# The attention output's transposition: TensorE and a copy, or a transposing DMA

## The chip, the cores and the metric

The kernel runs on one core of a Trainium2 chip. The metric is the device time of one execution, in microseconds, and smaller is better. The time before is 302.44 us, the median of three runs (302.19 to 304.47).

## The reference

Inputs are `q`, `k`, `v` of shape 4 x 8 x 768 x 64 (batch, head, position, channel), a small `sort_net` of 4 x 8 x 8 x 8, and the weights of a feed-forward layer. The 768 positions of a head are 8 blocks of 96. Attention runs inside a block; keys and values are first mixed across blocks by a matrix `P`.

```python
P = sort_net
for _ in range(5):
    P = exp(P - max(P, -1)); P = P / sum(P, -1); P = P / sum(P, -2)
k_sorted = einsum('bhij,bhjcd->bhicd', P, k_blocks)
v_sorted = einsum('bhij,bhjcd->bhicd', P, v_blocks)
scores = q_block @ k_sorted_block.T / sqrt(64)
attn   = softmax(scores)
x      = (attn @ v_sorted_block)          # rearranged to 3072 tokens x 512
h      = x @ w_in                         # 512 -> 2048
g      = max(h, 0) + alpha * min(h, 0)
out    = g @ w_out                        # 2048 -> 512, float32
```

## The kernel before

There are 32 attention steps `g`, one for each batch and block, and each step treats 96 tokens for all 8 heads. Batch `b` owns steps 8b to 8b+7. Before a batch can start, its queries, keys and values are loaded by GpSimd's queue (`load_q`, `load_k`, `load_v`), transposed or mixed on TensorE (`prep_q`, `prep_k`, `prep_v`) and copied out of PSUM; values also pass a rearranging copy (`conv_v`). The feed-forward weights come over the same GpSimd queue at the start, between batch 0's and batch 1's data.

One attention step (the function `attention`) is a chain. `s1` (L522) makes the scores, VectorE takes their negated row maximum `nm` (L527), `s2` (L535 and L540) makes the scores again with the maximum subtracted, ScalarE takes the exponential `Esb` (L546), and `o` (L554) multiplies by the values, with a column of ones that gives the row sums. VectorE takes the reciprocals `rec` (L559) and writes the normalised result `xq` (L562): 96 tokens on partitions, 512 channels in bf16 beside one another, 1,024 bytes in a row. There are two buffers of `xq`, used in turn.

The feed-forward layer wants channels on partitions. So four TensorE transposes (L571), one for each group of 128 channels, write into the free half of the first bank of `psO`, and one copy on ScalarE or VectorE (the line of the helper `copy`, L312) moves 128 x 384 elements into `xT`. `xT` holds four planes of 3,072 tokens, and step `g` fills 96 columns of each plane.

The feed-forward layer works on chunks of steps: (0,1), (2,3), and then four at a time. For each chunk `ffn1` runs 16 times, once for each 128 rows of the hidden layer: four matmuls (L591) into one of two banks `psH`, ScalarE's relu of the negated value into `t1` (L599), and VectorE's sum of the two parts into `hT` (L602). `ffn2` (L623) then makes 128 tokens of output at a time from 16 matmuls of 512 columns, a copy goes to one of four buffers `outstg`, and SyncE stores it (L633). In the before version SyncE does nothing else after two small loads at the start.

The order of all instructions is fixed when the kernel is built. A planner (`_Graph`) is given each operation with its engine, an estimated duration, a priority and the buffers that it reads and writes. It walks forward in estimated time, gives each free engine the ready operation of lowest priority number, and so writes one queue for each engine; ready means that the operations it depends on have ended in the estimate, plus a latency for a change of engine. The queues are then emitted in that order with semaphore waits. On the chip each engine works its queue strictly in that order, so an operation whose input is late holds all that stand behind it. An operation marked `EITHER` goes to whichever of ScalarE and VectorE is free first.

Attention step `g` has priority `g`. `ffn1` of the chunk that ends before step `gb` starts at priority `gb` + 0.5. For a DMA from SyncE the planner reckons 100 ns for the issue, 700 ns to the start, the given duration, and 500 ns to the end:

```python
free[e] = at + (600 if e == "pool" else 100)
begin = max(dma_free if e == "pool" else 0, free[e] + 700)
...
op.end = begin + dur + (1500 if e == "pool" else 500)
```

A buffer written again waits for those who still read it: `xq` of step `g` + 2 waits for whoever reads `xq` of step `g`.

Of the kernel before, what the change touches and what calls it, by code (L numbers as in the profile page):

```python
# [7 lines left out]
AP = bass.AP  # L8
# [4 lines left out]
B, H, S, D = 4, 8, 768, 64  # L13
NB = 8
BLK = S // NB
NT = B * S
DM = H * D
DFF = 2048
KT_TILES = DM // 128
# [11 lines left out]
def t_pe(*mms):  # L31
    return sum(max(n, m, 64) / 2.4 + 4 for n, m in mms)


def t_act(n):
    return 170 + n / 1.2


def t_dve(n, mode=1):
    return 155 + n / (0.96 * mode)  # L40
# [195 lines left out]
def bass_sinkhorn_attn__then__act_prelu_kernel(  # L236
# [11 lines left out]
    G = _Graph()  # L248
    sems = {e: es.enter_context(nc.semaphore("s_" + e)) for e in ENGS}

    def dma_sem(name):
        return [es.enter_context(nc.semaphore("d_" + name)), 0]

    def sb(name, shape, dt):
        return es.enter_context(nc.sbuf_tensor(name, shape, dt))
# [4 lines left out]
    PE, ACT, DVE, POOL, SYNC = ("pe",), ("act",), ("dve",), ("pool",), ("sync",)  # L260
    PSP = [("psP", 0), ("psP", 1)]
    EITHER = ("act", "dve")

    identf = sb("identf", [128, 128], F32)
    identb = sb("identb", [128, 128], BF16)
# [18 lines left out]
    xT = sb("xT", [128, KT_TILES, NT], BF16)  # L284
# [11 lines left out]
    xq = [sb("xq%d" % n, [96, 512], BF16) for n in range(2)]  # L296
# [9 lines left out]
    psOb = psO.bitcast(BF16)  # L306
# [4 lines left out]
    def copy(e, o, i):  # L311
        return e.activation(o, i, ACTF.Copy) if e is nc.scalar else e.tensor_copy(o, i)  # L312

    def t_either(n, mode=1):
        return {"act": t_act(n), "dve": t_dve(n, mode)}
# [3 lines left out]
          w=["P"], prio=-100, dma=(dma_sem("sn"), 0))  # L319
# [187 lines left out]
              prio=prio)  # L507


    def attention(g, prio):  # L510
        b, i = g // NB, g % NB
        n, m = b % 2, g % 2
        kt_keys = [("KT", n, u) for u in range(6)]
        qt_keys = [("QTz", n, u, x, y) for u in range(3) for x in range(2) for y in range(2)]
        vs_keys = [("VS", n, u) for u in range(8)]
        banks_s, banks_o = ["psS0", "psS1"], ["psO0", "psO1"]

        def s1(e):
            inst = None
            for s in range(8):  # L520
                h4, hp = s // 2, s % 2
                inst = e.matmul(AP(psS, (s // 4) * 512 + (s % 4) * 96, [[1024, 96], [1, 96]]),  # L522
                                AP(QTz[n], hp * 3072 + h4 * 768 + i * 96, [[6144, 128], [1, 96]]),
                                AP(KT[n], h4 * 768 + i * 96, [[3072, 128], [1, 96]]))
            return inst
        G.add(PE, s1, t_pe(*[(96, 96)] * 8), r=kt_keys + qt_keys, w=banks_s, prio=prio)
        G.add(DVE, lambda e: e.tensor_reduce(  # L527
            AP(nm[m], 0, [[8, 96], [4, 2], [1, 4]]), AP(psS, 0, [[1024, 96], [512, 2], [96, 4], [1, 96]]),
            AxisListType.X, AluOpType.max, negate=True), t_dve(768), r=banks_s, w=[("nm", m)], prio=prio)

        def s2(e):
            inst = None
            for h4 in range(4):
                base = (h4 // 2) * 512 + (h4 % 2) * 192
                e.matmul(AP(psS, base, [[1024, 96], [1, 192]]),  # L535
                         AP(KT[n], h4 * 768 + i * 96, [[3072, 128], [1, 96]]),
                         AP(QTz[n], h4 * 768 + i * 96, [[6144, 128], [3072, 2], [1, 96]]),
                         start=True, stop=False)
                for hp in range(2):
                    inst = e.matmul(AP(psS, base + hp * 96, [[1024, 96], [1, 96]]),  # L540
                                    AP(nm[m], 2 * h4 + hp, [[8, 96], [0, 96]]),
                                    AP(identb, 0, [[128, 96], [1, 96]]), start=False, stop=(hp == 1))
            return inst
        G.add(PE, s2, t_pe(*[(192, 96), (96, 96), (96, 96)] * 4), r=kt_keys + qt_keys + [("nm", m), "identb"],
              w=banks_s, prio=prio)
        G.add(ACT, lambda e: e.activation(  # L546
            AP(Esb[m], 0, [[768, 96], [384, 2], [1, 384]]), AP(psS, 0, [[1024, 96], [512, 2], [1, 384]]),
            ACTF.Exp, scale=0.125), t_act(768), r=banks_s, w=[("Esb", m)], prio=prio)

        def o(e):  # L550
            inst = None
            for s in range(8):
                h4, hp = s // 2, s % 2
                inst = e.matmul(AP(psO, hp * 512 + h4 * 68, [[1024, 96], [1, 65]]),  # L554
                                AP(Esb[m], s * 96, [[768, 96], [1, 96]]),
                                AP(VS[n], ((hp * 4 + h4) * 8 + i) * 65, [[64 * 65, 96], [1, 65]]))
            return inst
        G.add(PE, o, t_pe(*[(65, 96)] * 8), r=vs_keys + [("Esb", m)], w=banks_o, prio=prio)
        G.add(DVE, lambda e: e.reciprocal(AP(rec[m], 0, [[8, 96], [4, 2], [1, 4]]),  # L559
                                          AP(psO, 64, [[1024, 96], [512, 2], [68, 4]])), 200,  # L560
              r=banks_o, w=[("rec", m)], prio=prio)
        G.add(DVE, lambda e: e.tensor_tensor(  # L562
            out=AP(xq[m], 0, [[512, 96], [256, 2], [64, 4], [1, 64]]),
            in0=AP(psO, 0, [[1024, 96], [512, 2], [68, 4], [1, 64]]),
            in1=AP(rec[m], 0, [[8, 96], [4, 2], [1, 4], [0, 64]]), op=AluOpType.mult), t_dve(512),
            r=banks_o + [("rec", m)], w=[("xq", m)], prio=prio)

        def tr(e):
            inst = None
            for kt in range(4):  # L570
                inst = e.matmul(AP(psOb, 640 + kt * 96, [[2048, 128], [1, 96]]),  # L571
                                AP(xq[m], kt * 128, [[512, 96], [1, 128]]),
                                AP(identb, 0, [[128, 96], [1, 96]]), is_transpose=True)
            return inst
        G.add(PE, tr, t_pe(*[(96, 128)] * 4), r=[("xq", m), "identb"], w=["psO0"], prio=prio)
        o2 = AP(xT, b * S + i * BLK, [[KT_TILES * NT, 128], [NT, 4], [1, 96]])
        i2 = AP(psOb, 640, [[2048, 128], [96, 4], [1, 96]])
        G.add(EITHER, lambda e: copy(e, o2, i2), t_either(384, 2), r=["psO0"], w=[("xT", g)], prio=prio)


    step = [0]

# [77 lines left out]
    for p in range(2):  # L660
# [6 lines left out]
          r=["alphaR", "identf"], w=PSP, prio=-44)  # L667
    G.add(DVE, lambda e: e.tensor_scalar(out=omaT[:, :], in0=AP(psP, 0, [[512, 128], [1, 16]]), scalar1=-1.0,
                                         scalar2=1.0, op0=AluOpType.mult, op1=AluOpType.add), 200,
          r=PSP, w=["omaT"], prio=-44)  # L670
# [4 lines left out]
    for ga, gb in chunks:  # L675
        w = gb - ga
# [11 lines left out]
    for g in range(NG + 12):  # L688
        while fp < len(ffn_plan) and ffn_plan[fp][0] < g:
            pr, kind, a = ffn_plan[fp]  # L690
            if kind == 0:
                ffn1(*a, pr)
            else:
                ffn2(*a)
            fp += 1
        if g >= NG:
            continue
        b, i = g // NB, g % NB
        if i == 0 and b + 1 < B:
            load_k(b + 1, 8 * b - 20)  # L700
            if b != 2:
                load_v(b + 1, 8 * b - 19)
            if b == 1:
                load_v(3, 8 * b - 17)
            load_q(b + 1, 8 * b - 18)
        attention(g, g)
        if b + 1 < B:
            units = ([(prep_k, u) for u in range(6)] + [(prep_q, u) for u in range(3)]
                     + [(conv_v, u) for u in range(8)] + [(prep_v, u) for u in range(8)])
            for x in range(len(units)):  # L710
                if i == 1 + x * 7 // len(units):
                    units[x][0](b + 1, units[x][1], 8 * b + 2 + x * 5 / len(units))
# [49 lines left out]
```

## Time and profile before

| what | value |
|---|---|
| median of the runs | 302.44 us |
| span of the profiled execution | 300.7 us, 1.7 us less than that median |
| mean granted TensorE clock | 0.949 of full |
| 128 transposes (L571), TensorE busy | 11.3 us, mean 213 ns of one with its drain |
| 32 copies psO to xT | 22 on VectorE at 352 ns, 10 on ScalarE at 490 ns |
| 24 stores from SyncE (L633), 256 KB each | 2.0 us from issue to landing (median) |
| two small loads from SyncE, 8 KB each | 1.6 us from issue to landing |

The page gives each engine's busy time, then the span in 40 slices of about 7.5 us with one digit for each. TensorE's matmuls are pipelined, so the duration of one contains its drain; what a group of matmuls takes from the queue is the distance from its first start to the start of the group behind it. The span runs from the first instruction to the last one, and the 1.7 us around it are taken as fixed.

A table of stretches gives, for each engine, the busy time inside the stretch and the number of instructions, then the granted TensorE clock, the share of the 16 DMA engines that were busy, and the rate. A timeline row gives start, duration, engine, line, operation, what is written and read, and in brackets the idle time before it and who ended it.

### The profile page before, as it was taken

How to read it: one execution, taken by the hardware profiler on the slowest of the kernel's cores; microseconds unless marked ns; L12 is line 12 of the kernel's file. 1: busy time of each engine (PE TensorE's matmuls, PEld its weight loads, DVE VectorE, ACT ScalarE, POOL GpSimd, SP SyncE). 2: the span in 40 equal slices, each digit the busy share in tenths (PEclk: the TensorE clock that was granted, in tenths of full speed). 3: DMA queues.
4: the chain of work that ended last, by engine and by line, in shares of the span. 5: the costliest groups of instructions: out<-in, count | busy, mean ns of one | idle time of the engine just before them, and what ended most of it. 6: DMA issues, size and time to landing. Idle time of an engine off the chain costs nothing.

```text
span 300.7 us, 6668 instructions
## 1 busy us (share of the span) xinstructions
PE 280.1 (93%) x2932; PEld 194.3 (65%) x2932; DVE 192.1 (64%) x372; ACT 174.3 (58%) x300; POOL 11.8 (4%) x23
## 2 busy tenths in 40 slices
PE   5959999866979998999999999999999999999995
PEld 5948988645856766666666666676666666655542
DVE  7894377687764586867656767675666566654410
ACT  3696323999796659765445586655444544444421
POOL 8301000001000000000000000000000000000000
PEclk9995557999979999999999999999999999999999
DMA  6999999746700100010001101101010001010011
GB/s 115 211 206 191 213 216 215 147 86 106 161 2 35 37 3 0 2 37 33 4 35 38 37 0 37 37 0 37 35 38 35 2 35 37 35 37 35 35 73 70
DMA packets 9229, 20.37 MB, mean 68 GB/s; under 512 B 736, under 2 KB 4848, under 8 KB 8944
## 3 DMA queue, kind: packets, MB, share of 16 engines
q0 software_dynamic: 5664, 13.63, 24.4%
q1 hardware_dynamic: 3536, 6.31, 5.6%
q8 instruction: 23, 0.38, 0.5%
q14 instruction: 6, 0.05, 0.1%
HBM read 27.28 MB, written 6.29 MB: 112 GB/s over the span
## 4 chain that ended last, share of the span: by engine, by line
PE 78%; ACT 11%; DVE 9%; issue 1%
PE psH L591 25%; PE psY L623 22%; ACT QTz L312 4%; PE psS L535 4%; PE psS L540 4%; PE psS L522 4%; PE psP L498 4%; PE psO L554 4%; PE psS L623 3%; ACT VD L312 3%; PE psP L468 2%; DVE QTz L353 2%; PE psO L571 2%; DVE QTz L312 1%; ACT t L599 1%
## 5 line engine op out<-in xcount | busy, mean ns | idle before, releaser
L602 DVE SCALAR_TENSOR_TENSOR hT<-t,omaT,psH 128x384 bf16<-128x384 f32 (+1 forms) x144 | 80.3, 566 | 57.2 <-ACT t L599 56.4
L591 PE MATMUL psH<-xT,w_in_bf 128*128 128x384 bf16 (+1 forms) x576 | 102.4, 311 | 2.7 <-DVE hT L602 2.6
L599 ACT ACTIVATE t<-psH 128x384 f32<-128x384 f32 (+1 forms) x144 | 64.1, 453 | 55.0 <-PE psH L591 53.9
L623 PE MATMUL psY<-w_out_bf,hT 128*128 128x512 bf16 x336 | 86.7, 382 | 0.0
L591 PEld LDWEIGHTS psH<-xT,w_in_bf 128*128 128x128 bf16 x576 | 50.3, 100 | 26.4 <-DVE hT L602 4.8
L623 PEld LDWEIGHTS psY<-w_out_bf,hT 128*128 128x128 bf16 x336 | 31.2, 99 | 27.2 <-issue 0.6
L546 ACT ACTIVATE Esb<-psS 96x768 bf16<-96x768 f32 x32 | 25.8, 806 | 26.7 <-PE psS L540 26.4
L527 DVE TENSOR_REDUCE nm<-psS 96x8 bf16<-96x768 f32 x32 | 30.4, 951 | 7.6 <-PE psS L522 6.3
L535 PE MATMUL psS<-QTz,KT 128*96 128x192 bf16 x128 | 27.1, 264 | 0.8 <-DVE nm L527 0.8
L540 PE MATMUL psS<-identb,nm 96*96 96x96 bf16 x256 | 27.0, 216 | 0.0
L540 PEld LDWEIGHTS psS<-identb,nm 96*96 96x96 bf16 x256 | 25.7, 133 | 1.8
L562 DVE TENSOR_TENSOR xq<-psO,rec 96x512 bf16<-96x512 f32 x32 | 22.0, 687 | 1.1
L312 ACT ACTIVATE VD<-VST 64x768 bf16<-64x768 bf16 (+1 forms) x14 | 20.6, 1518 | 0.1
L554 PEld LDWEIGHTS psO<-VS,Esb 96*96 96x96 bf16 x256 | 17.1, 133 | 4.9 <-issue 0.5
L312 ACT ACTIVATE QTz<-psP 64x512 bf16<-64x512 bf16 x25 | 18.8, 753 | 1.9 <-PE psP L445 1.6
L719 PE MATMUL psY<-identb 128*128 128x128 bf16 x199 | 16.7, 254 | 3.3 <-ACT identb L312 3.3
L535 PEld LDWEIGHTS psS<-QTz,KT 128*96 128x96 bf16 x128 | 16.8, 131 | 4.0 <-DVE nm L527 1.1
L522 PEld LDWEIGHTS psS<-KT,QTz 128*96 128x96 bf16 x256 | 16.5, 133 | 3.9 <-ACT Esb L546 0.5
L522 PE MATMUL psS<-KT,QTz 128*96 128x96 bf16 x256 | 18.2, 218 | 0.4 <-ACT Esb L546 0.4
L312 ACT ACTIVATE VS<-psP 96x512 bf16<-96x512 f32 x18 | 12.3, 682 | 10.6 <-PE psP L498 10.3
L554 PE MATMUL psO<-VS,Esb 96*96 96x65 bf16 x256 | 17.5, 215 | 0.0
L719 PEld LDWEIGHTS psY<-identb 128*128 128x128 bf16 x199 | 14.5, 116 | 3.8 <-ACT identb L312 3.3
(75 smaller groups left out, 228.8 us busy)
## 6 DMA issues: line engine op xcount, KB each, us to landing
out_dram<-outstg SPq DMA_DIRECT2D x24, 256.0 KB, 2.0
QS<-in_q_dram POOLq DMA_DIRECT2D x4, 768.0 KB, 25.0
KS<-in_k_dram POOLq DMA_DIRECT2D x4, 768.0 KB, 21.0
VST<-in_v_dram POOLq DMA_DIRECT2D x4, 768.0 KB, 23.5
w_in_bf<-in_moe_w_in_dram POOLq DMA_DIRECT2D x4, 512.0 KB, 18.2
w_out_bf<-in_moe_w_out_dram POOLq DMA_DIRECT2D x2, 1024.0 KB, 28.3
P<-in_sort_net_dram SPq DMA_DIRECT2D x1, 8.0 KB, 1.6
alphaR<-in_moe_alpha_dram SPq DMA_DIRECT2D x1, 8.0 KB, 1.6
```

Source lines behind the costliest of these rows:

```text
L312: return e.activation(o, i, ACTF.Copy) if e is nc.scalar else e.tensor_copy(o, i)
L522: inst = e.matmul(AP(psS, (s // 4) * 512 + (s % 4) * 96, [[1024, 96], [1, 96]]), AP(QTz[n], hp * 3072 + h4 * 768 + i * 96, [[6144, 128], [ ...
L527: G.add(DVE, lambda e: e.tensor_reduce(AP(nm[m], 0, [[8, 96], [4, 2], [1, 4]]), AP(psS, 0, [[1024, 96], [512, 2], [96, 4], [1, 96]]), Axis ...
L535: e.matmul(AP(psS, base, [[1024, 96], [1, 192]]), AP(KT[n], h4 * 768 + i * 96, [[3072, 128], [1, 96]]), AP(QTz[n], h4 * 768 + i * 96, [[61 ...
L540: inst = e.matmul(AP(psS, base + hp * 96, [[1024, 96], [1, 96]]), AP(nm[m], 2 * h4 + hp, [[8, 96], [0, 96]]), AP(identb, 0, [[128, 96], [1 ...
L546: G.add(ACT, lambda e: e.activation(AP(Esb[m], 0, [[768, 96], [384, 2], [1, 384]]), AP(psS, 0, [[1024, 96], [512, 2], [1, 384]]), ACTF.Exp ...
L554: inst = e.matmul(AP(psO, hp * 512 + h4 * 68, [[1024, 96], [1, 65]]), AP(Esb[m], s * 96, [[768, 96], [1, 96]]), AP(VS[n], ((hp * 4 + h4) * ...
L591: inst = e.matmul(AP(psH, hb * 512, [[1024, 128], [1, n]]), AP(w_in_bf, kt * DFF + ft * 128, [[KT_TILES * DFF, 128], [1, 128]]), AP(xT, kt ...
L599: G.add(ACT, lambda e: e.activation(AP(t1[tb], 0, [[384, 128], [1, n]]), AP(psH, hb * 512, [[1024, 128], [1, n]]), ACTF.Relu, scale=-1.0), ...
L602: G.add(DVE, lambda e: e.scalar_tensor_tensor(out=AP(hT, ft * RING + tok % RING, [[FT_TILES * RING, 128], [1, n]]), in0=AP(t1[tb], 0, [[38 ...
L623: inst = e.matmul(AP(bank[0], bank[1], [[row, 128], [1, 512]]), AP(hT, ft * RING + tok % RING, [[FT_TILES * RING, 128], [1, 128]]), AP(w_o ...
L719: inst = e.matmul(psY[:, 0:128], identb[:, :], identb[:, :])
```

## The change

The four transposes and the copy of each step go, and one transposing DMA issued by SyncE takes `xq` to `xT` directly. Its estimated duration in the planner is 1,300 ns. Two semaphores, one for each `xq` buffer, tell of the landing.

```diff
+    d_x = [dma_sem("x%d" % n) for n in range(2)]
+
     def attention(g, prio):
...
-        def tr(e):
-            inst = None
-            for kt in range(4):
-                inst = e.matmul(AP(psOb, 640 + kt * 96, [[2048, 128], [1, 96]]),
-                                AP(xq[m], kt * 128, [[512, 96], [1, 128]]),
-                                AP(identb, 0, [[128, 96], [1, 96]]), is_transpose=True)
-            return inst
-        G.add(PE, tr, t_pe(*[(96, 128)] * 4), r=[("xq", m), "identb"], w=["psO0"], prio=prio)
-        o2 = AP(xT, b * S + i * BLK, [[KT_TILES * NT, 128], [NT, 4], [1, 96]])
-        i2 = AP(psOb, 640, [[2048, 128], [96, 4], [1, 96]])
-        G.add(EITHER, lambda e: copy(e, o2, i2), t_either(384, 2), r=["psO0"], w=[("xT", g)], prio=prio)
+        G.add(SYNC, lambda e: e.dma_start_transpose(
+            AP(xT, b * S + i * BLK, [[KT_TILES * NT, 128], [NT, 4], [1, 96]]),
+            AP(xq[m], 0, [[512, 96], [1, 512]])),
+            1300, r=[("xq", m)], w=[("xT", g)], prio=prio, dma=(d_x[m], 0))
```

The DMA moves 96 x 512 elements of two bytes, 96 KB, from SBUF to SBUF. `ffn1` now waits for its landing, SyncE waits for `xq` before issuing it, and `xq` of step `g` + 2 waits for the landing of step `g`'s.

## The prediction

> **What bounds the kernel now.** I read the page's busy times and slices first, then the table of stretches, then timelines around the transposition, and last the landings.
>
> ```profile
> PE 280.1 (93%) x2932; PEld 194.3 (65%) x2932; DVE 192.1 (64%) x372; ACT 174.3 (58%) x300; POOL 11.8 (4%) x23
> ...
> PE   5959999866979998999999999999999999999995
> ...
> PEclk9995557999979999999999999999999999999999
> DMA  6999999746700100010001101101010001010011
> ```
>
> TensorE (PE) is the limit from slice 13 on, about 98 us: 24 of the 32 steps lie there. The first 13 slices are different. The DMA row is at 9 while attention begins, and TensorE's clock is at half until about 49 us. The stretches:
>
> ```profile
> 42.00:48.00 6.00, 5.64 (x50) 5.18 (x50) 4.21 (x13) 1.47 (x3) 0.00 (x0) 0.50 0.99 204
> 48.00:54.00 6.00, 6.00 (x96) 4.96 (x95) 4.44 (x12) 3.42 (x9) 0.00 (x0) 0.91 1.06 218
> 54.00:60.00 6.00, 4.71 (x92) 3.68 (x92) 3.43 (x7) 5.63 (x9) 0.00 (x0) 1.00 0.62 131
> 60.00:62.80 2.80, 2.55 (x48) 1.59 (x42) 2.53 (x5) 2.74 (x6) 0.00 (x0) 1.00 0.00 0
> 62.80:70.00 7.20, 4.81 (x60) 3.81 (x61) 5.96 (x12) 7.12 (x8) 0.56 (x1) 1.00 0.61 112
> ```
>
> The columns are PE, PEld, DVE, ACT and POOL busy, granted clock, DMA share, GB/s. The loads queued by GpSimd keep the 16 DMA engines full until just before 60 us; then the share is 0.00 until the next load. In 42 to 54 TensorE is busy for 11.6 of 12 us, so a hold there is lost time. From 62.8 to 70 ScalarE is the full engine.
>
> **What is removed.** A group of four transposes in the steady part:
>
> ```profile
> 207.68 1.47 PE L591 MATMUL psH<-xT,w_in_bf 128*128 128x384 bf16 x8
> 208.98 0.34 PE L571 MATMUL psO<-identb,xq 96*128 96x96 bf16 x4
> 209.15 0.60 PE L623 MATMUL psY<-w_out_bf,hT 128*128 128x512 bf16 x2
> ```
>
> From start to start it takes 0.17 us of TensorE's queue, not the 0.34 of its busy time, which contains the drain. At half clock the groups at 39.2 and 43.6 take 0.45 and that at 48.6 takes 0.32. The sum is 29 x 0.17 + 0.45 + 0.45 + 0.32 = 6.1 us, all on the path, because the queue there is full or nearly so. The copies are 22 x 0.352 + 10 x 0.490 = 12.6 us of VectorE and ScalarE; in the steady part both have idle time (64% and 58% busy), so that is worth nothing there. In the stretches from 62.8 to 92 where ScalarE is full, one ScalarE copy of 0.49 falls (at 61.8, its edge): I take 0.5 us, bounds 0 to 1.5 if the planner can also move other `EITHER` copies away from ScalarE. The gain is 6.6 us, bounds 6.1 to 7.6.
>
> **What is added, with quiet DMA engines.** One issue by SyncE per step, and a landing. Nothing in the trace transposes by DMA. The nearest rows are SyncE's own transfers: 1.6 us from issue to landing for 8 KB, 2.0 us for 256 KB. The 96 KB lie between in size. The mean packet of SyncE's queue takes 76 ns (5.6% of 16 engines' 300.7 us, 3,536 packets). A store has 128 rows, 8 packets per engine. If `xq` goes as 96 rows of 1,024 bytes, that is 6 per engine, and 1.6 to 2.0 us stand. If each row is cut at every 128 channels, as `xT`'s four planes suggest, there are 384 pieces of 256 bytes, 24 per engine, and 16 more than a store's 8 cost 16 x 0.076 = 1.2 us: 3.2 us. I take 3.2, bounds 1.6 to 3.2 for these forms. Who waits? From the end of a chunk's last `xq` to the first `ffn1` of the chunk the trace has 2.5 us for chunk (4..7), 3.4 for the last chunk and 5.6 to 8.6 for the others with four steps. The planner now reckons 100 + 700 + 1300 + 500 = 2,600 ns and 220 for changes of engine, 2.8 us, where transposes (229 ns), copy (355) and changes of engine (490) were 1.1, so it puts the first `ffn1` some 1.7 us later in TensorE's order and fills with `ffn2` and attention: 4.2 and 5.1 us are then available. At 3.2 us nothing waits. That cover is gone above 4.2 us; at 6 us two chunks would lose 1.8 + 0.9 = 2.7 us.
>
> [...]
>
> On SyncE a transposing DMA that waits for `xq` holds the stores behind it, and a store that waits for `outstg` holds the transposition behind it. Stores take 0.33 us to issue, lie 7 us or more apart, and have four buffers, and the planner orders both by the same clock; I count nothing, and up to 1 us per chunk is inside the cover above. VectorE's `xq` of step g + 2 waits for the landing of step g, with `hT` and `nm` queued behind it: in the steady part that is two periods of 6.8 us against 3.2, nothing.
>
> **What is added, with busy DMA engines.** This decides. The transpositions of steps 0 to 3 (`xq` ends at 38.5, 43.0, 47.4 and 51.5) meet full DMA engines:
>
> ```profile
> q0 software_dynamic: 754, 4.63, 93.3%
> ```
>
> That is 36 to 60 us: 0.933 x 16 x 24 us / 754 packets = 0.475 us for a packet of the loads. What it does to SyncE's queue is seen once, in the first store, issued at 72.6 us beside two loads:
>
> ```profile
> DMA to landing us min/median/max: 2.0/2.0/9.1
> ```
>
> The excess of 7.1 us over its 8 packets per engine is 0.89 us each. If a packet of SyncE's queue lets one load packet pass each time, it is at least 0.475. So a transposition of 6 rows per engine lands after 2.0 + 6 x 0.475 = 4.9 to 2.0 + 6 x 0.89 = 7.3 us. One of 24 pieces lands after 3.2 + 24 x 0.475 = 14.6 to 3.2 + 24 x 0.89 = 24.6 us, and step 1's stands behind step 0's.
>
> Who waits is the first chunk's `ffn1`:
>
> ```profile
> 42.29 0.69 DVE L562 TENSOR_TENSOR xq<-psO,rec 96x512 bf16<-96x512 f32 x1
> ...
> 46.03 1.47 PE L591 MATMUL psH<-xT,w_in_bf 128*128 128x192 bf16 x8
> ```
>
> Step 1's `xq` is ready at 43.0 and the first `ffn1` starts at 46.0. With the planner's 1.7 us it moves to about 47.7, behind which `s2`, `o` and all of TensorE's queue stand. With 6 rows, step 1 lands at 47.9 to 50.3 and the hold is 0.2 to 2.6 us. With 24 pieces, step 0 is not done before 38.6 + 14.6 = 53.2 and step 1 not before the loads have drained, just under 60 us plus a microsecond: landing at about 60, a hold of 12.3 us, bounds 8 to 14. VectorE's `xq` of step 2 (46.7) waits for step 0 inside the same hold. Little is won back: ScalarE soon stands at a relu or an exponential that needs TensorE, and later stretches are full. Step 4 on is after the drain. The loads of 62.8 to 82.5 meet steps 5 and 6, whose chunk starts only at 93.9, after step 7, with the engines quiet: hidden.
>
> I take 24 pieces, since the destination's planes cut every row at 128 channels, and 12.3 us.
>
> **Sum.** 300.7 - 6.6 + 12.3 = 306.4 us of span, and with the 1.7 us around it 308.1. I shade the hold by 1 us for what ScalarE does meanwhile: 307.
>
> **Rivals.** (1) Whole rows travel as one packet, or pieces are gathered: the hold is 1.4 us, and 300.7 - 6.6 + 1.4 + 1.7 = 297.2 us, range 295.5 to 299.3; up to a landing of 6.5 us after step 1's `xq` the change stays faster by over 1%. For it: the store's 2 KB rows went as one packet each. Against it: the planes of `xT`. (2) The hold is 4 to 9 us, because the loads' turns are shared more kindly or ScalarE's full stretch absorbs some: 300 to 305. (3) Quiet latency is far larger, above the 6.8 us period, and SyncE becomes the bound: at 10 us the chunks lose what exceeds their cover (with the 1.7 us: 4.2, 5.1, 7.3 three times, 9.8, 10.3), 5.8 + 4.9 + 3 x 2.7 + 0.2 = 19 us, 315 before the start's hold is added. (4) It isn't a transposition in hardware but element by element: 49,152 / 16 = 3,072 packets per engine at 76 ns, 233 us for each of 32, thousands of us. Nothing speaks for it but that no row excludes it.
>
> **Chances.** 24 pieces 0.45 (303 to 311), rival 1 0.37, rival 2 0.13, rivals 3 and 4 0.05. The range 295.5 to 311 leaves out about 0.12 and the tails of the two main cases; the likeliest case alone is 303 to 311. About 1% is what a measurement tells from no change, 299.4 to 305.5. Faster 0.38, same 0.15, slower 0.47.
>
> **What would show it.** TensorE's first `ffn1` of chunk (0,1) starts near 60 us with an idle gap of some 12 us before it that a DMA into `xT` ended; the landings of steps 0 and 1 are over 14 us, those after 100 us near 3. The distance between steady steps falls from 6.77 to 6.60. I am wrong if landings under load stay below 8 us (rival 1), or if the steady `ffn1` waits for `xT` (rival 3).

## The result and the profile after

The changed kernel takes 312.73 us (median of four runs, 312.48 to 314.19) against 302.43 before: a ratio of 1.036, 95% interval 1.031 to 1.040. The direction was as forecast, but the size was not: 307.0 was predicted, and 312.7 lies above the range's end of 311. The profiled execution has a span of 310.9 us, 10.2 more than before.

The page's busy times, and the rows of the slices for TensorE, its clock and the DMA engines:

```profile
PE 270.8 (87%) x2768; PEld 188.3 (61%) x2804; DVE 188.5 (61%) x353; ACT 167.8 (54%) x287; POOL 11.8 (4%) x23
...
PE   5979950198589799889999999999999999999995
...
PEclk9975555589979999999999999999999999999999
DMA  6999999600883020011111110111101211110011
```

TensorE is busy for 9.3 us less (some of that is records missing from this trace: L617 has 301 matmuls to 336 weight loads), and there is a hole that was not there: the digits 0 and 1 in slices 6 and 7, counted from 0, where the DMA row is still at 9 and 6. The stretches, with the columns as before, show how complete it is:

```profile
42.00:48.00 6.00, 1.73 (x13) 1.53 (x13) 1.10 (x5) 0.81 (x1) 0.00 (x0) 0.50 1.02 193
48.00:54.00 6.00, 0.00 (x0) 0.00 (x0) 0.00 (x0) 0.00 (x0) 0.00 (x0) 0.50 1.02 206
54.00:60.00 6.00, 0.00 (x0) 0.00 (x0) 0.00 (x0) 0.00 (x0) 0.00 (x0) 0.50 0.88 184
60.00:62.80 2.80, 1.66 (x15) 1.61 (x16) 0.19 (x1) 0.33 (x1) 0.00 (x0) 0.50 0.02 2
```

For 12 us no compute engine does anything; only the DMA engines work (share 1.02 and 0.88). TensorE's timeline names what ended it:

```profile
43.49 0.36 PE L542 MATMUL psS<-identb,nm 96*96 96x96 bf16 x2
43.78 0.28 PE L659 MATMUL psP<-identf,alphaR 16*128 16x16 f32 x1
61.14 0.82 PE L585 MATMUL psH<-xT,w_in_bf 128*128 128x192 bf16 x4 [17.07 <-DMA xT<-xq]
61.75 0.34 PE L556 MATMUL psO<-VS,Esb 96*96 96x65 bf16 x2
```

The first `ffn1` (now L585) stands at the head of the queue from 44.07 and waits 17.07 us for the landing in `xT`; `o` of step 2 (L556) stands behind it though its input was ready at 44.7, when this row of ScalarE ends:

```profile
43.89 0.81 ACT L548 ACTIVATE Esb<-psS 96x768 bf16<-96x768 f32 x1 [4.33 <-PE psS L542]
```

The instructions of the transposing DMA, with the landings:

```profile
L570 SPq DMA_TRANSPOSE xT<-xq x32: 1179/1181/1911, 37.9 to 272.6; - x32
...
DMA to landing us min/median/max: 2.3/2.3/19.6
```

The median landing is 2.3 us after issue. Steps 0 and 1 took 16.8 and 19.6 us: issued at 37.9 and 41.5, landed at 54.7 and 61.1. The DMA table from 42 to 56 us shows why:

```profile
q0 software_dynamic: 475, 2.72, 96.0%
q1 hardware_dynamic: 476, 0.11, 6.6%
```

The columns are packets, MB and the share of the 16 engines. The loads moved 475 packets and SyncE's queue 476, in lots of 6 KB and 0.2 KB: packet for packet they alternate, 14 x 16 / 475 = 0.47 us for each turn. On the page packets under 512 bytes rose from 736 to 14,048, that is by 416 for each of 32 DMAs: 384 pieces of 256 bytes and 32 of 4 bytes. Each piece of 128 channels is a packet, 24 for each of the 16 engines if they share alike, and the first of step 0 went out 3.9 us after the issue.

In the steady part the distance from one step's `s1` to the next fell from 6.77 to 6.60 us. Before, and then after:

```profile
243.85 0.52 PE L522 MATMUL psS<-KT,QTz 128*96 128x96 bf16 x8
250.62 0.39 PE L522 MATMUL psS<-KT,QTz 128*96 128x96 bf16 x5
```

```profile
247.18 0.52 PE L524 MATMUL psS<-KT,QTz 128*96 128x96 bf16 x8
253.78 0.43 PE L524 MATMUL psS<-KT,QTz 128*96 128x96 bf16 x6
```

So 17.1 us were lost in one hold, and 6.9 gained elsewhere: 17.1 - 6.9 = 10.2. The 6.9 is a remainder and not a measurement, and 0.7 of it was there before any transposition: step 0's `xq` began at 37.18 in this execution and at 37.85 in the one before.

Executions of one and the same kernel differ by several microseconds and in their mean clock (all runs of the kernel before lay between 295.5 us, at a clock of 0.964, and 304.5 us, at 0.944), so the ratios below are against runs of the kernel before on the same chip, and a single run tells a hold from no hold, not two per cent.

### The profile page after: what moved, and what is told of

It reads as the page before. It is cut to its first block, busy times and chain, and to the rows that moved or that the text cites. A ratio compares the mean times of both kernels' runs of the same rounds, so it can differ in the third digit from the quotient of the medians.

```text
span 310.9 us, 6403 instructions
## 1 busy us (share of the span) xinstructions
PE 270.8 (87%) x2768; PEld 188.3 (61%) x2804; DVE 188.5 (61%) x353; ACT 167.8 (54%) x287; POOL 11.8 (4%) x23
## 2 busy tenths in 40 slices
DMA packets 22539, 23.49 MB, mean 76 GB/s; under 512 B 14048, under 2 KB 18160, under 8 KB 22256
## 4 chain that ended last, share of the span: by engine, by line
PE 71%; ACT 14%; DMA 6%; DVE 6%; issue 2%
PE psH L585 25%; PE psY L617 21%; DMA xT<-xq 6%; ACT VD L312 6%; PE psO L556 4%; ACT QTz L312 3%; PE psS L617 3%; PE psP L498 3%; PE psS L524 3%; PE psS L537 3%; PE psS L542 3%; DVE QTz L353 2%; PE psP L468 1%; ACT t L593 1%; PE psY L713 1%
## 5 line engine op out<-in xcount | busy, mean ns | idle before, releaser
L585 PE MATMUL psH<-xT,w_in_bf 128*128 128x384 bf16 (+1 forms) x576 | 103.0, 311 | 19.2 <-DMA xT<-xq 17.1
L617 PE MATMUL psY<-w_out_bf,hT 128*128 128x512 bf16 x301 | 79.2, 381 | 2.3 <-issue 0.5
L585 PEld LDWEIGHTS psH<-xT,w_in_bf 128*128 128x128 bf16 x576 | 50.3, 100 | 44.8 <-DMA xT<-xq 17.2
L617 PEld LDWEIGHTS psY<-w_out_bf,hT 128*128 128x128 bf16 x336 | 32.0, 99 | 29.1 <-issue 0.6
L561 DVE RECIPROCAL rec<-psO 96x8 f32<-96x8 f32 x32 | 6.4, 201 | 23.9 <-PE psO L556 23.4
L556 PEld LDWEIGHTS psO<-VS,Esb 96*96 96x96 bf16 x256 | 16.9, 132 | 5.7 <-ACT Esb L548 1.9
L312 ACT ACTIVATE QTz<-psP 64x512 bf16<-64x512 bf16 x24 | 18.1, 756 | 1.9 <-PE psP L445 1.6
L556 PE MATMUL psO<-VS,Esb 96*96 96x65 bf16 x256 | 17.7, 216 | 0.6 <-ACT Esb L548 0.5
L312 ACT ACTIVATE outstg<-psY 128x512 f32<-128x512 f32 x20 | 11.9, 597 | 9.8 <-PE psY L617 9.7
```

The lines of the kernel that those rows point to most:

```text
L585: inst = e.matmul(AP(psH, hb * 512, [[1024, 128], [1, n]]), AP(w_in_bf, kt * DFF + ft * 128, [[KT_TILES * DFF, 128], [1, 128]]), AP(xT, kt ...
L617: inst = e.matmul(AP(bank[0], bank[1], [[row, 128], [1, 512]]), AP(hT, ft * RING + tok % RING, [[FT_TILES * RING, 128], [1, 128]]), AP(w_o ...
```

## The experiments

**Is it the first steps alone?** Steps 0 to 3 keep the TensorE transposes and the copy.

```diff
+        if g in range(0, 4):
+            G.add(PE, tr, ...)
+            G.add(EITHER, lambda e: copy(e, o2, i2), ...)
+            return
         G.add(SYNC, lambda e: e.dma_start_transpose(
```

> Steps 0 to 3 keep the four TensorE transposes and the copy; the other 28 steps use the transposing DMA. Theory (the loss is one hold of TensorE, 17.1 us, by the first two transposing DMAs that land among the loads; all else is a gain of 6.9 us): no gap of TensorE that a DMA into xT ends above 1 us, and 302.4 less 28 x 0.17 to 0.22 = 296 to 298 us. Rival (the new order of the queues costs time by itself, in the stretches where ScalarE is full): 302 us or more though the hold is gone.

Measured: 295.5 us against 299.4 before on that chip (medians), ratio 0.979 (0.966 to 0.992). Of TensorE's waits, the two longest are these (total, times, longest):

```profile
PE psY L726 <- ACT identb L312: 3.3, 1, 3.3
PE psH L598 <- DVE hT L609: 3.2, 6, 1.8
```

No wait for a DMA into `xT` is in the list. Against `after`, four steps of 32 are worth some 17 us (ratios 1.036 and 0.979). The new order by itself costs nothing that can be seen, so that rival falls.

**Is it the loads, or the transposing DMA being slow early on?** All 32 steps use it, and the loads of batches 1 to 3 wait for step 1's landing.

```diff
-              load_us, w=[("QS", b % 2)], prio=prio, dma=(d_q[b % 2], 0))
+              load_us, r=[("xT", 1)] * (b > 0), w=[("QS", b % 2)], prio=prio, dma=(d_q[b % 2], 0))
...
         attention(g, g)
+        if g == 1:
+            loads()
```

(The same for `KS` and `VST`.)

> All 32 steps use the transposing DMA, but the loads of q, k and v of batches 1 to 3 are issued only after the landing of step 1's transposition, so the DMA engines are quiet for steps 0 and 1. Theory (the loads' packets delay it): steps 0 and 1 land 2.3 to 3 us after issue, the first ffn1 starts at 44 to 45 us, and the kernel takes 295 to 303 us, with steps 2 and 3 landing after 10 to 17 us in its place. Rival (a transposing DMA is slow early in the kernel for a reason of its own, such as its first use): steps 0 and 1 land after 14 us or more again, and the kernel takes 310 us or more.

The DMA table from 36 to 43 us has both transpositions, and the landings are quiet ones:

```profile
q0 software_dynamic: 24, 0.02, 1.8%
...
xT<-xq SPq DMA_TRANSPOSE x2, 2.3
```

The first `ffn1` started at 42.8 us without a wait, so the cause is the loads. The time was 307.0 us against 299.4, ratio 1.022 (1.013 to 1.031), worse than the 295 to 303 expected: the loads now fill the DMA engines from 44 to 73 us and meet steps 2, 3 and 4 (landings of 19.8, 26.3 and 12.4 us). The waits:

```profile
PE psH L585 <- DMA xT<-xq: 7.3, 1, 7.3
...
DVE xq L564 <- DMA xT<-xq: 7.1, 1, 7.1
```

The second chunk's `ffn1` waits 7.3 us, and before that VectorE waits 7.1 us to write `xq` of step 4 over that of step 2, which holds TensorE for 6.8 us more through `hT`. The hold had moved, and the second wait of the prediction's list (the reuse of `xq`) came to count.

**Does the number of pieces count?** Steps 0 and 1 transpose one plane of four, and the other three planes of these tokens hold zeros.

```diff
+        wide = 1 if g < 2 else 4
         G.add(SYNC, lambda e: e.dma_start_transpose(
-            AP(xT, b * S + i * BLK, [[KT_TILES * NT, 128], [NT, 4], [1, 96]]),
-            AP(xq[m], 0, [[512, 96], [1, 512]])),
+            AP(xT, b * S + i * BLK, [[KT_TILES * NT, 128], [NT, wide], [1, 96]]),
+            AP(xq[m], 0, [[512, 96], [1, 128 * wide]])),
```

> The DMAs of steps 0 and 1 transpose only the first 128 of 512 channels, a quarter of the pieces; the other three planes of these 192 tokens hold zeros set by GpSimd at the start, and the matmuls run as before. Left out: three quarters of the transposition of steps 0 and 1. Theory (each piece takes a turn of 0.60 us with the loads): 6 pieces per engine land after 5 to 7 us each, the hold is 3 to 5 us, the kernel takes 298 to 302 us. Rival (what SyncE issues there lands only when the loads have drained, however small): landing after 17 and 20 us, 311 to 313 us.

The landings were 10.2 and 8.4 us and the hold 6.1, between the two expectations, and nearer to the theory's. In 40 to 45 us:

```profile
q0 software_dynamic: 133, 1.01, 99.0%
q1 hardware_dynamic: 122, 0.02, 6.3%
```

Again the packets alternate, at 5 x 16 / 133 = 0.60 us a turn. What the theory had left out is the wait before the first packet, 3.8 us here: 3.8 + 6 x 0.60 = 7.4, and 1 to 3 us for the end. From 24 pieces to 6 the landing falls by 6.6 to 11.2 us, so it is turns and not only the drain of the loads. (The planner put GpSimd's zeroing early, and TensorE began at 10.6 us and not 3.3, so the whole time of 303.2 us is not compared.)

**Is the transposition itself to blame?** Steps 0 and 1 copy the same rows in 384 plain pieces. If the number of pieces decides, as the experiment before has it, they land as late as with the transposing DMA.

```diff
+        if g < 2:
+            G.add(SYNC, lambda e: e.dma_start(
+                AP(xT, b * S + i * BLK, [[KT_TILES * NT, 96], [NT, 4], [1, 96]]),
+                AP(xq[m], 0, [[512, 96], [128, 4], [1, 96]])),
+                1300, r=[("xq", m)], w=[("xT", g)], prio=prio, dma=(d_x[m], 0))
+            return
```

> The DMAs of steps 0 and 1 are plain copies of the same 96 rows in 384 pieces of 192 bytes, without a transposition, to the same four planes (set to zero at the start). Left out: the transposition of steps 0 and 1. [...] Rival (the transposition itself is what suffers beside other traffic): landing after 4 to 10 us, 298 to 304 us.

```profile
L571 SPq DMA_DIRECT2D xT<-xq x2: 597/670/742, 40.2 to 45.6; - x2
...
DMA to landing us min/median/max: 15.3/15.4/15.4
```

A plain copy in as many pieces lands after 15.4 and 15.3 us, where the transposing DMAs took 16.8 and 19.6, and the hold is 13.0 us. The transposition as such is not what suffers: from 44.5 to 56 us the loads moved 412 packets and SyncE's queue 413. (The time was 313.6 us, with the same late start of TensorE.)

**Is it the place in the queue?** The planner is given durations near the real ones for steps 0 to 3, with four buffers of `xq`, and then with the two there were.

```diff
-            1300, r=[("xq", m)], w=[("xT", g)], prio=prio, dma=(d_x[m], 0))
+            {0: 15500, 1: 18300, 2: 15000, 3: 11000}.get(g, 1300), r=[("xq", m)], w=[("xT", g)], prio=prio, dma=(d_x[m], 0))
```

> All 32 steps use the transposing DMA. The planner is given durations of 15.5, 18.3, 15 and 11 us for steps 0 to 3, near what they take on the chip, and there are four buffers of xq in place of two, each with its semaphore. Theory (the hold is in the place of the first ffn1 in TensorE's queue, ahead of work that could run): landings of steps 0 and 1 stay over 14 us, TensorE's gap that a DMA into xT ends falls from 17 us to under 3, the ratio to before is 0.98 to 1.00. Rival (the work of the start hangs on the landing whatever the order, since little else is ready): the gap stays above 8 us, ratio above 1.01.

> As the kernel with four buffers and longer planned durations, but with the two buffers of xq. Theory (a second wait stands behind the first: xq of step 2 waits for the landing of step 0 at about 54 us): VectorE waits there, TensorE runs out of work before it for 5 to 10 us, 302 to 309 us. Rival (only the place of ffn1 matters): no gap above 3 us, 294 to 300 us.

With four buffers no wait for a landing is left although steps 0 and 1 still land after 16.7 and 18.9 us; ratio 0.984 (0.969 to 0.998). With two buffers a single run gave 294.0 us and a wait of 1.0 us on TensorE and 1.1 on VectorE:

```profile
DVE xq L564 <- DMA xT<-xq: 1.1, 1, 1.1
...
PE psH L585 <- DMA xT<-xq: 1.0, 1, 1.0
```

The second wait that I expected there did not come, since the planner, told the truth, also puts `xq` of step 2 later in VectorE's queue. Timed in twelve more runs, the same kernel was slower than in that one:

> The kernel with the longer planned durations and two buffers of xq, timed. It took 294.0 us in one look with 1.0 us of TensorE waiting for a landing in xT. Theory (the removal brings 6 to 7 us when nothing waits for the landings): ratio to before 0.97 to 0.985. Rival (that one look was a lucky one, and the waits of VectorE behind step 0's landing cost what the theory first said): ratio 0.99 or more.

It took 300.5 us, ratio 0.997 (0.993 to 1.000). That is the rival's number but not its reason: no engine waits for a landing in this profile. The clock row of the single run, and then that of the timed kernel's profile:

```profile
PEclk9968955589999999999999999999999999999999
```

```profile
PEclk9975555558999999999999999999999999999999
```

These are the same instructions, in the second execution at half clock from slice 3 to 8 (counted from 0), in the first with the clock nearly open in slices 3 and 4. Of the 6.8 us between the two spans, 5.1 lie ahead of step 0's `xq` and 6.2 ahead of step 1's, where the clocks differ. The twelve timed runs had mean clocks of 0.909 to 0.925, the single one 0.947. So the order removes the hold, which is shown. That the rest of its gain hangs on the clock is argued: the timed kernel's granted clock is still 0.51 from 60 to 70 us, and that of the kernel before is 1.00 from 50 to 80 us.

**How many steps need TensorE?** Two, and eight, in place of four.

> Steps 0 and 1 alone keep TensorE's transposes and the copy. Theory (only the first chunk's landing holds TensorE long; steps 2 and 3 land at about 61 us when the loads have drained, before their ffn1 at 66, and hold VectorE's xq of step 4 for about 3 us): ratio 0.98 to 0.995. Rival (the holds of later steps are as costly): ratio above 1.0.

> Steps 0 to 7 keep TensorE's transposes and the copy, so that every transposing DMA has quiet DMA engines. Theory (24 steps x 0.17 us and little else): 4 to 5 us less than before, ratio 0.983 to 0.988. Rival (the copies taken from ScalarE and VectorE in the stretch from 60 to 92 us matter as well): slower than the kernel with four steps on TensorE by over 1%.

> Steps 0 and 1 on TensorE, timed beside the reordered kernel. Theory: both lie within 1% of each other, 0.975 to 0.99 of before. Rival: the reordered kernel is slower by over 1%, since 32 landings and not 30 hang on the loads.

With two steps the ratio is 0.985 (0.976 to 0.994), and 0.984 (0.977 to 0.990) when timed again in six runs, 296.6 us. With eight it is 296.8 us against 302.5 (medians of four and seven runs). The three mixed kernels lie within 0.5% of one another, so VectorE's and ScalarE's share of the copies is not seen. With two, steps 2 and 3 landed after 12.5 and 8.8 us (18.1 and 14.1 in the second profile), and their chunk did not wait; VectorE waited 2.4 us (7.4 in the second) to write `xq` of step 4. At mean clocks of 0.942 to 0.949 this kernel took 295.2 to 297.3 us in seven runs and the kernel before 301.3 to 304.5, so the gain is there at equal clock too. Against the four quickest of the 17 runs of the kernel before beside the second timing (295.5 to 299.4 us, clocks of 0.960 to 0.966) the gain is only 0.5%, so it is not a clear 2%. The reordered kernel is 1.3% slower than the mixed one beside it, which is the rival's side; the rival's reason, the landings, is again not what its profile shows.

**Is the clock at the start worth microseconds by itself?** The kernel before, with the idle matmuls that fill planned gaps up to 36 us of the plan and not 26.

```diff
-    G.fill(warm, 56, ident_op, 26e3)
+    G.fill(warm, 56, ident_op, 36e3)
```

> The kernel before, with TensorE's transposes, and the idle matmuls that fill planned gaps at the start up to 36 us of planned time in place of 26. Theory (the clock at the start is worth microseconds by itself, and its opening depends on how densely TensorE works): it opens before 49 us, ratio to before 0.97 to 0.99. Rival (the start is set by the chain of attention steps, not by the clock): 0.995 to 1.005.

The median of four runs was 303.3 us against 302.4, so in most runs the filling did not open the clock sooner. But one of the four took 295.4 at a mean clock of 0.983, the other three 303.3 to 303.7 at 0.943 to 0.949. In the profiled one, of the three:

```profile
30.00:40.00 10.00, 10.00 (x95) 9.22 (x94) 4.44 (x11) 2.80 (x4) 0.00 (x0) 0.50 1.20 216
40.00:50.00 10.00, 10.00 (x101) 9.37 (x100) 5.11 (x15) 1.99 (x4) 0.00 (x0) 0.55 1.02 205
```

TensorE is shown busy for all of 20 us, and the granted clock stays at half. What opens it is not shown; the runs of this kernel show only that a higher mean clock goes with some 8 us less. Whether idle matmuls would help the reordered or the mixed kernel was not measured.

## Why the prediction was right in kind and wrong in size

**What is removed**, right: 6.6 us predicted, 6.9 found as the difference between the hold and the loss, or 6.2 without the 0.7 that this execution was ahead at step 0, and 0.17 us per step in the steady part, as read from start to start. (The prediction's 64% and 58% are of the whole span; from 170 to 264 us VectorE is busy for 68% and ScalarE for 53%, which changes nothing.)

**The added DMA, quiet**, right: 2.3 us, inside the bounds of 1.6 to 3.2 though not the 3.2 that was taken; no steady chunk waits, and the last one has a gap of 0.6 us, since its landing took 3.8. Stores do not always lie 7 us or more apart as the prediction has it (3.4 to 4.1 us at the end), which cost nothing here. The 2.3 us for 96 KB stand beside 2.0 for a store of 256 KB.

**The added DMA, among the loads**, right: 24 pieces, landings over 14 us, step 1 landing when the loads had drained. Taking turns was the mechanism, shown by nearly equal packet counts in `after` (475 and 476) and in the two kernels with fewer (133 and 122) or plain pieces (412 and 413). One term was missing: the first packet went out 3.9 us after the issue, where it took 1.2 us in the experiment with the loads late. That 16.8 us still fell within 14.6 to 24.6 is luck in part, since the price of a turn was at its lower bound (0.47 us) and made room for it. Rival 1, whole rows or gathered pieces, is refuted by the 384 packets.

**The hold**, wrong in size: 12.3 us in the prediction (shaded to some 11.3), 17.1 measured. The step that failed is the sentence that the first `ffn1`, with the planner's 1.7 us, "moves to about 47.7". It stood at the head of TensorE's queue at 44.1. I had moved it by the difference of two latencies in a plan that otherwise stayed as it was. In the planner's own figures, worked out anew for both kernels, the first `ffn1` starts at 32.73 us before and at 32.79 after: without the transposes in the bank of `psO`, `o` of step 1 goes ahead of `s1` of step 2, step 1's `xq` ends at 29.97 and not 30.95, and that takes up most of the longer latency. What stood ahead of `ffn1` before (`s1` of step 3 and `o` of step 2) is now behind it. On the chip, before:

```profile
44.72 0.88 PE L522 MATMUL psS<-KT,QTz 128*96 128x96 bf16 x8 [0.36 <-ACT Esb L546]
45.40 0.81 PE L554 MATMUL psO<-VS,Esb 96*96 96x65 bf16 x8
46.03 0.83 PE L591 MATMUL psH<-xT,w_in_bf 128*128 128x192 bf16 x4
```

TensorE's queue at this place, the kernel before and then after (the groups of `s2` are left out):

```
before: alphaR, s1 (step 3), o (step 2), ffn1, ...
after:  alphaR, ffn1, o (step 2), ffn1, s1 (step 3), ...
```

That is 3.6 of the missing microseconds (0.7 of them this execution's earlier start, which the gain has too). The landing at 61.1 and not 60 is 1.1, and the microsecond that I took off for work in the meantime was not there: the table shows all compute engines idle. Together 3.6 + 1.1 + 1.0 = 5.7, against a miss of 312.7 - 307.0 = 5.7, and the 0.3 more of gain is nearly made up by roundings. The hold's upper bound of 14 us had no term for the place, and so the range ended too low.

**The reuse of `xq`** was put inside the same hold; in `after` it did cost nothing of its own, but it cost 6.8 us of TensorE's time when the loads were moved.

## What to carry to other kernels

A small transfer that sits on a dependency chain must be priced by what shares the DMA engines at that moment, not by its quiet latency: here 2.3 us became 16.8 and 19.6, since step 0's first packet went out after 3.9 us and each of an estimated 24 small packets per engine (384 on 16) took a turn of 0.47 us with a 6 KB packet of a bulk load. Where a planner fixes the order, a wrong duration can cost far more than itself, since the queue is held by the late operation with ready work behind it: 17.1 us here, and at most 1.0 with durations near the real ones. And when an operation is taken out, the plan must be made again before one says where the waiting instruction stands. Leaving the first two or four steps to TensorE turned a loss of 3.6% into a gain of about 1.5 to 2.1%, with intervals from 0.6 to 3.4%, and less against the quickest runs of the kernel before.

## What the runs showed that was not expected

- A transposing DMA of 96 x 512 bf16 occupies SyncE for 1.18 us (a store: 0.33) and is 384 packets of 256 bytes and 32 of 4 bytes.
- In `after`, the first packet of a transposing DMA went out 3.9 us after the issue in step 0, with the loads filling the engines, 4.4 us in step 4, with a DMA share of 0.80 by the loads, and 1.2 us in 27 of the other steps. Why is not shown.
- Two executions of one kernel (the two-buffer one with longer planned durations) ran at 292.2 and 299.0 us of span with mean granted clocks of 0.947 and 0.913. In the kernel before with more idle matmuls, 20 us of full TensorE rows, as far as rows that contain each matmul's drain can tell, went at a clock of 0.50 to 0.55. What opens the clock is not shown.
